# Attention, experts and feed-forward on one core: the two halves of a pair's weighted sum as one group, and the work before the first scores spread over other engines

## The chip, the core and the metric

The kernel runs on one core of a Trainium2 chip. A core has TensorE (PE, matmuls, and transposes as matmuls with the identity; its weight loads are shown as PEld), VectorE (DVE), ScalarE (ACT), GpSimd (POOL) and SyncE (SP, which here only issues DMAs). Each engine works through its own row of instructions in order and waits at semaphores for the others. Matmul results go to PSUM, eight banks of 2 KB in each of 128 partitions. The metric is the device time of one execution in microseconds, less is better. It is about 0.2% exact for this kernel.

## What is computed

Inputs are q, k, v of shape 4 x 8 x 576 x 64 (batch, heads, positions, head size) and s of 4 x 8 x 576, all float32. Cut to what matters:

```python
cum = np.cumsum(np.maximum(s, 0.0), axis=-1)
bias = np.minimum(-(cum[:, :, :, None] - cum[:, :, None, :]), 0.0)
scores = np.where(causal, -1e9, q @ k.transpose(0, 1, 3, 2) / 8 + bias)
attn = np.exp(scores - scores.max(-1, keepdims=True))
x = (attn / (attn.sum(-1, keepdims=True) + 1e-9)) @ v      # attention
x = x.transpose(0, 2, 1, 3).reshape(2304, 512)
e = argmax(x @ w_gate)             # one of 8 experts for each row of x
y = gate_w * sigmoid(x @ w_output_gate)[e] * (relu(x @ w1[e]) @ w2[e])
out = relu(y @ w_in)**2 @ w_out    # a third feed-forward layer
```

## The kernel before

Attention goes through 16 pairs of heads, four pairs to a batch. The 576 positions are four blocks of 128 rows and a tail of 64. A pair has seven units of work, which the list `order=[0, 1, 3, 11, 2, 10, 4]` puts into a row: units 0 and 1 are the first and the second row block of both heads, 2 and 3 the third and fourth block of the first head, 10 and 11 those of the second head, and 4 is the tail of both heads (the "tail scores", in a PSUM tile `s2` of two banks; all the others have tiles of one bank). Each unit goes through the same steps: scores on PE (`emit_s`, L635), bias, mask and the row maximum in one VectorE instruction (`emit_m`, L662), exp and row sum on ScalarE (`emit_e`, L679), transposes of the probabilities on PE (`emit_t`, L695, tile `t`), and a copy of them to SBUF on ScalarE or VectorE (`emit_v`, L714 and L716), into `pt0` for rows 0 to 255 and `pt1` for the rest.

Then comes the weighted sum with v, `emit_pv` (L732), which puts the two heads side by side (64 output partitions each, the form 128*64 in the profile). Half 0 sums the rows 0 to 255 over two blocks of keys: per head 256 and 128 columns. Half 1 sums the other 320 rows over five blocks: three times 320, then 192 and 64 columns. A float32 matmul shows as two instructions. Each half has a PSUM bank of its own from the ring of three banks that the transposes use too (tag `t`). ScalarE copies each half out (`emit_ov`, L743, into `oT`), VectorE makes the reciprocals of the row sums (`emit_rc`, L759 and L761), PE transposes the result back (`emit_xt`, L770), and VectorE scales it (`emit_xe`, L805) into a buffer that is stored to DRAM as x (`store_x`, L870 and L874).

Meanwhile the next pairs are prepared: q and k are loaded by six DMAs for each pair (L511, L514), transposed in three parts on PE (`qk_pe`, L548 and L550), converted to a high half on ScalarE (`qk_hi`, L575) and a low half on VectorE (`qk_lo`, L579), copied on GpSimd, and moved to the upper partitions by DMAs (L583). From the third pair on the bias comes in as extra rows of the scores' operands, read from the DRAM buffer `aug_d` (L538). The first two pairs add it by a fourth matmul with `cum_k` and `cum_q`, four slices that are made at the start from the cumulative sum (L1177 on ScalarE, L1179 on VectorE). Once a batch the gate's logits are made by `emit_lm` (L827), half by half, and the steps of the choice of the expert (L896 to L944) run between the attention steps of the following pairs.

The order of all this on each engine is written out by hand: `at(key, fn, ...)` puts a step into a list that is sorted by its key, in units of one seventh of a pair, and the table `K_` has the keys. `pv=[[3.74, 3.87], [8.47, ...]]` places half 0 in the middle of the next pair's units and half 1 near the end of them. The other keys that matter here are those of the copy after a half (`ov`), of its reciprocals (`rc`), of its transposes (`xt`), its scaling (`xe`), the store (`sx`) and the logits (`lt`).

Of the kernel before, what the change touches and what calls it, by code (L numbers as in the profile page):

```python
# [12 lines left out]
F32 = mybir.dt.float32  # L13
# [11 lines left out]
P = 128  # L25
# [17 lines left out]
    lt=[[-0.37, -0.33, 0.07, 0.12], [-0.22, 0.14, 0.64, 0.96]],  # L43
# [17 lines left out]
    pv=[[3.74, 3.87], [8.47, 8.49, 8.51, 8.53, 8.57]],  # L61
# [6 lines left out]
    sx=2.42,  # L68
# [22 lines left out]
def attention_moe_ffn_kernel(  # L91
# [359 lines left out]
    with tc.manual_schedule():  # L451
        with ExitStack() as actx:
# [34 lines left out]
            pt0 = [apool.tile([P, 2, 2, 256], F32, name=f"pt0{a}") for a in range(K_["ptb"])]  # L487
# [18 lines left out]
            def load_qk(pp):  # L506
                b, j = divmod(pp, HP)
                t = raw_q[pp] = qk_p.tile([P, 2 * QM + 2 * D], F32, tag="qk", name="qk")
                for i, src in enumerate((q, k)):
                    for hd in range(2):  # L510
                        nc.sync.dma_start(  # L511
                            out=t[:, i * QM:(i + 1) * QM].rearrange("p (r h d) -> p r h d", h=2, d=D)[:, :, hd],
                            in_=src[b, 2 * j + hd, 0:S - TAIL, :].rearrange("(r p) d -> p r d", p=P))
                    nc.sync.dma_start(  # L514
# [183 lines left out]
            def emit_v(pp, u, act):  # L698
                pb = pp % K_["ptb"]
                j0 = 0  # L700
                for i, (tp, n) in enumerate(t_t.pop((pp, u))):
                    if u < 2:
                        src = tp[:, 0:n * P].rearrange("p (h j i) -> p h j i", h=2, i=P)
                        dst = pt0[pb][:, :, 0:u + 1, u * P:(u + 1) * P]
# [15 lines left out]
            def emit_pv(pp, half, jbs):  # L720
                vt = raw_v[pp]
                if jbs[0] == 0:
                    o_t[pp, half] = ps_o.tile([P, 512], F32, tag=o_tag, name=o_tag)
                o = o_t[pp, half]
                last = 1 if half == 0 else NB - 1
                pt = (pt0 if half == 0 else pt1)[pp % K_["ptb"]]
                n = 256 if half == 0 else S - 256
                base = 0 if half == 0 else 2
                for jb in jbs:
                    c0 = max(jb - base, 0) * P  # L730
                    for hd in range(2):
# [3 lines left out]
                            rhs=pt[:, hd, jb, c0:n],  # L735
# [15 lines left out]
            def emit_rc(pp, half):  # L751
# [4 lines left out]
                b0, b1 = (0, 2) if half == 0 else (2, NB)  # L756
# [350 lines left out]
            with tc.tile_pool(name="prep", bufs=1) as prep:  # L1107
# [21 lines left out]
                nc.vector.tensor_copy(out=mask[:, 3 * P:4 * P], in_=mf)  # L1129
                for hd in range(2):  # L1130
                    r = slice(64 * hd, 64 * hd + 64)
                    nc.vector.tensor_copy(out=mask_t[r, S - TAIL:S], in_=mf[r, 64 * hd:64 * hd + 64])
# [8 lines left out]
                nc.scalar.copy(out=st_a[0][64:128, 0:3:2], in_=zf[64:128].unsqueeze(1).to_broadcast([64, 2, S]))  # L1141
                nc.vector.tensor_reduce(
# [34 lines left out]
                nc.scalar.activation(out=cum_q[:, 0], in_=cum_r.bitcast(F32), func=AF.Copy, scale=sel[:, 0:1])  # L1177
                for r in range(1, 2 * ND):
                    nc.vector.tensor_scalar(  # L1179
# [640 lines left out]
```

## Time and profile before

| | us |
|---|---|
| median of 3 runs | 862.26 (862.01 to 862.64) |
| the profiled execution | 862.62 |
| its span, first to last instruction | 860.9 |
| TensorE busy in it | 841.9 (98%) |
| VectorE busy | 523.8 (61%) |
| ScalarE busy | 450.7 (52%) |
| GpSimd busy | 260.0 (30%) |

The profile is of one execution. The span and the runs differ by the start and the end of the program around it. Busy shares are means over very different stages: attention in the first quarter, where all engines work, and the experts and the feed-forward layer behind it, which are mostly matmuls.

### The profile page before, as it was taken

What the parts mean: (1) busy time and instruction counts of PE and PEld (TensorE: products, weight loads), DVE (VectorE), ACT (ScalarE), POOL (GpSimd) and SP (SyncE); (2) the same over time, 40 slices, a digit from 0 to 9 for tenths busy, and PEclk for the clock granted to TensorE, in tenths of its full rate; (3) what the DMA queues carried; (4) which work ended last, traced back from release to release, by engine and by line L of the source; (5) the groups of instructions that cost most, each with busy time, mean ns of one, the idle gap of its engine ahead of it and who ended that gap; (6) DMA issues with size and microseconds to landing.
All of it is one profiled execution on the core that took longest, in us unless ns stands there. A gap on an engine that the chain in (4) does not pass through costs nothing.

```text
span 860.9 us, 15163 instructions
## 1 busy us (share of the span) xinstructions
PE 841.9 (98%) x5412; PEld 747.3 (87%) x5412; DVE 523.8 (61%) x1186; ACT 450.7 (52%) x1008; POOL 260.0 (30%) x302
## 2 busy tenths in 40 slices
PE   7999999999999999999999999999999999999996
PEld 5877777767799999999999999999999999999995
DVE  8667778877767686777976667664233343232221
ACT  6688888887555556565655546443233232232221
POOL 4312335534216555567422232331001011001001
PEclk9999999999999999999999999999999999999998
DMA  6667677753187978999983433321010121001001
GB/s 155 143 154 156 137 182 175 170 138 101 53 287 247 246 241 264 252 283 273 301 240 105 147 110 110 91 93 62 11 63 37 37 75 38 1 1 37 0 1 40
DMA packets 113028, 113.14 MB, mean 131 GB/s; under 512 B 66033, under 2 KB 83953, under 8 KB 112946
## 3 DMA queue, kind: packets, MB, share of 16 engines
q1 hardware_dynamic: 106162, 96.97, 41.6%
q0 software_dynamic: 3664, 9.62, 3.2%
q10 hardware_dynamic: 3120, 5.51, 1.9%
q8 instruction: 45, 0.74, 0.4%
q14 instruction: 37, 0.30, 0.1%
HBM read 80.50 MB, written 23.32 MB: 121 GB/s over the span
## 4 chain that ended last, share of the span: by engine, by line
PE 56%; issue 30%; ACT 5%; DVE 4%; POOL 2%; DMA 1%; POOLq 1%; SPq 1%; ACTq 0%; DVEq 0%
PE z L1427 19%; PE z L1469 11%; PE z L1478 7%; PE t L732 5%; PE s L635 5%; PE t L695 4%; ACT p L679 2%; POOL out_dram L1537 1%; ACT sta L575 1%; PE z L333 1%; PE t L548 1%; ACT pt L714 1%; PE s L770 1%; POOLq L1545 1%; PE t L827 1%
## 5 line engine op out<-in xcount | busy, mean ns | idle before, releaser
L1427 PE MATMUL z<-xt,w 128*128 128x384 f32 (+6 forms) x1920 | 329.6, 320 | 0.1
L1427 PEld LDWEIGHTS z<-xt,w 128*128 128x128 f32 x1920 | 308.1, 188 | 9.0 <-DVE h L1438 0.4
L1478 PE MATMUL z<-w,h 128*128 128x512 f32 x864 | 214.9, 393 | 0.0
L1478 PEld LDWEIGHTS z<-w,h 128*128 128x128 f32 x864 | 160.7, 188 | 29.3
L1447 DVE SCALAR_TENSOR_TENSOR r<-z,r 128x384 f32<-128x384 f32 x96 | 53.3, 555 | 127.4 <-ACT r L1446 127.4
L1446 ACT ACTIVATE r<-z 128x384 f32<-128x384 f32 x96 | 47.2, 492 | 150.8 <-PE z L1427 149.7
L1469 PE MATMUL z<-h,w 128*128 128x304 f32 (+5 forms) x768 | 111.0, 293 | 0.2 <-DVE h L1438 0.2
L1469 PEld LDWEIGHTS z<-h,w 128*128 128x128 f32 x768 | 104.0, 189 | 0.6 <-DVE h L1438 0.4
L1395 POOL TENSOR_TENSOR cvm<-cvm,cva 128x512 f32<-128x512 f32 x32 | 44.2, 1381 | 168.1 <-DVE cva L1391 128.3
L1454 DVE TENSOR_TENSOR h<-r,h 128x384 fp32r<-128x384 f32 x96 | 61.0, 635 | 50.4 <-ACT h L1453 50.4
L1537 POOL DMA_INDIRECT out_dram<-ysb,tok_m x18 | 17.4, 969 | 245.5 <-ACT ysb L1524 183.2
L679 ACT ACTIVATE p<-p,nm 128x128 f32<-128x128 f32 (+3 forms) x144 | 84.2, 590 | 4.8 <-DVE nm L662 4.7
L1453 ACT CAST h<-r 128x384 fp32r<-128x384 f32 x96 | 49.3, 514 | 63.7 <-DVE r L1447 63.3
L662 DVE CUSTOM_DVE_ANT_0 p<-s,mask 128x128 f32<-128x128 f32 (+3 forms) x128 | 59.6, 485 | 29.3 <-PE s L635 28.2
L250 DVE TENSOR_TENSOR w<-stg,w 128x1024 fp32r<-128x1024 f32 x49 | 73.6, 1502 | 5.4 <-ACT w L246 5.4
L695 PE MATMUL t<-ident,p 128*128 128x128 f32 x400 | 69.3, 283 | 2.6 <-DVE sta L579 1.1
L246 ACT CAST w<-stg 128x1024 fp32r<-128x1024 f32 x49 | 51.4, 1049 | 20.0 <-POOL cvm L1396 17.3
L695 PEld LDWEIGHTS t<-ident,p 128*128 128x128 f32 x400 | 44.5, 141 | 18.8 <-ACT p L679 6.8
L596 POOL CAST stb<-sta 64x1152 fp32r<-64x1152 f32 x28 | 31.4, 1150 | 78.1 <-PE s L635 47.9
L1396 POOL TENSOR_TENSOR cvm<-cvs,cvm 128x512 f32<-128x512 f32 x32 | 54.1, 1690 | 2.5
L635 PE MATMUL s<-sta 128*64 128x288 f32 (+4 forms) x204 | 50.1, 343 | 3.4 <-DMA sta<-aug_d 1.2
L714 ACT COPY pt<-t 128x512 f32<-128x512 f32 (+1 forms) x94 | 47.0, 515 | 7.3 <-PE t L732 4.1
(242 smaller groups left out, 1022.8 us busy)
## 6 DMA issues: line engine op xcount, KB each, us to landing
stg<-in_moe_w_dram SPq DMA_DIRECT2D x42, 512.0 KB
cv<-in_moe_w_out_dram SPq DMA_DIRECT2D x16, 512.0 KB
stx<-in_moe_w_dram SPq DMA_DIRECT2D x14, 512.0 KB
cv<-in_moe_w_in_dram SPq DMA_DIRECT2D x14, 512.0 KB
xr<-yT_d SPq DMA_DIRECT2D x8, 768.0 KB
qk<-in_q_dram SPq DMA_DIRECT2D x32, 128.0 KB
qk<-in_k_dram SPq DMA_DIRECT2D x32, 128.0 KB
v<-in_v_dram SPq DMA_DIRECT2D x32, 128.0 KB
```

The source lines that it names most:

```text
L250: nc.vector.tensor_tensor(out=lo, in0=raw.pop(job), in1=hi.bitcast(F32), op=ALU.subtract)
L635: nc.tensor.matmul(ps[0:mw, d0:d0 + nn], lhsT=ql[r, m0:m0 + mw], rhs=kl[r, c0:c0 + nn], start=(i == 0 and (tail or n == 0)), stop=(done an ...
L662: nc.vector.tensor_tensor_reduce(out=dst, in0=src, in1=msk, scale=-1.0, scalar=3.0e38, op0=ALU.add, op1=ALU.min, accum_out=nm[:, c:c + 1])
L679: nc.scalar.activation(out=pt[:, cs], in_=pt[:, cs], func=AF.Exp, scale=-1.0, bias=nm[:, c:c + 1], accum_out=rs[:, r:r + 1])
L695: nc.tensor.transpose(tp[:, i * P:(i + 1) * P], pt[:, j0:j0 + P], ident)
L714: nc.scalar.copy(out=dst, in_=src)
L1396: nc.gpsimd.tensor_tensor(out=m, in0=sq, in1=m, op=ALU.add)
L1427: nc.tensor.matmul(ps[:, 0:n], lhsT=wa[:, zw, kk, fl * P:(fl + 1) * P], rhs=xt[:, zx, kk, 0:n], start=(i == 0), stop=(i == 3 * KD - 1))
L1447: nc.vector.scalar_tensor_tensor(out=gg, in0=ps[:, 0:TT], scalar=0.0, in1=gg, op0=ALU.max, op1=ALU.mult)
L1454: nc.vector.tensor_tensor(out=ht[:, 1], in0=gg, in1=ht[:, 0].bitcast(F32), op=ALU.subtract)
L1469: nc.tensor.matmul(y_acc[g][d][:, 0:n], lhsT=wb[:, zw, fl, d * P:(d + 1) * P], rhs=ht[:, zh, 0:n], start=(f == 0 and i == 0), stop=(f == n ...
L1478: nc.tensor.matmul(acc, lhsT=ht[:, zh, c * P:(c + 1) * P], rhs=wb[:, zw, fl, :], start=(first and i == 0), stop=(last and i == 2))
```

## The change

Three things are changed.

First, the weighted sum. For all pairs but the last, half 0 is summed directly before half 1, and both halves go into one tile of two banks, from the pool in which the tail scores have their tile (tag `s2`). The copies of both halves then follow each other, and the reciprocals of a pair are made in one go for all five blocks. Since `pt0` is now read later, there are two of them, used in turn, and each is packed: the pieces of 256 and 128 columns stand behind one another. The transposes of half 0's result are moved to the next pair (`x0=10.87`), the store follows both halves (`sx=3.9`), and the logits of both halves stand side by side (`lt`).

Second, the front. The three loads of the first pair's k are issued by ScalarE, not by SyncE. The casts that make the masks go from VectorE to ScalarE; of the four slices of `cum_q` ScalarE makes two, not one, GpSimd the other two, and VectorE, which made three, none.

Third, the low halves of the first pair's last part are made before the `cum_q` slices.

```diff
-    lt=[[-0.37, -0.33, 0.07, 0.12], [-0.22, 0.14, 0.64, 0.96]],
+    lt=[[-0.37, -0.33, 0.07, 0.12], [-0.36, 0.14, 0.64, 0.96]],
...
-    pv=[[3.74, 3.87], [8.47, 8.49, 8.51, 8.53, 8.57]],
+    x0=10.87,
+    pv=[[8.45, 8.46], [8.47, 8.49, 8.51, 8.53, 8.57]],
...
-    sx=2.42,
+    sx=3.9,
...
-            pt0 = [apool.tile([P, 2, 2, 256], F32, name=f"pt0{a}") for a in range(K_["ptb"])]
+            pt0 = [apool.tile([P, 2, 3 * P], F32, name=f"pt0{a}") for a in range(2)]
...
+                    eng = nc.scalar if i == 1 and pp == 0 else nc.sync
                     for hd in range(2):
-                        nc.sync.dma_start(
+                        eng.dma_start(
...
-                        src = tp[:, 0:n * P].rearrange("p (h j i) -> p h j i", h=2, i=P)
-                        dst = pt0[pb][:, :, 0:u + 1, u * P:(u + 1) * P]
+                        src = tp[:, 0:n * P].rearrange("p (h c) -> p h c", h=2)
+                        dst = pt0[pp % 2][:, :, u * P:(2 * u + 1) * P]
...
-                    o_t[pp, half] = ps_o.tile([P, 512], F32, tag=o_tag, name=o_tag)
+                    if pp == NPAIR - 1:
+                        o_t[pp, half] = ps_o.tile([P, 512], F32, tag=o_tag, name=o_tag)
+                    else:
+                        if half == 0:
+                            o_t[pp] = ps_2.tile([P, 1024], F32, tag="s2", name="s2")
+                        o_t[pp, half] = o_t[pp][:, 512 * half:512 * half + 512]
...
-                b0, b1 = (0, 2) if half == 0 else (2, NB)
+                b0, b1 = (0, 2) if half == 0 else (2 if pp == NPAIR - 1 else 0, NB)
...
-                nc.vector.tensor_copy(out=mask[:, 3 * P:4 * P], in_=mf)
-                for hd in range(2):
-                    r = slice(64 * hd, 64 * hd + 64)
-                    nc.vector.tensor_copy(out=mask_t[r, S - TAIL:S], in_=mf[r, 64 * hd:64 * hd + 64])
...
+                nc.scalar.copy(out=mask[:, 3 * P:4 * P], in_=mf)
+                for hd in range(2):
+                    r = slice(64 * hd, 64 * hd + 64)
+                    nc.scalar.copy(out=mask_t[r, S - TAIL:S], in_=mf[r, 64 * hd:64 * hd + 64])
...
-                nc.scalar.activation(out=cum_q[:, 0], in_=cum_r.bitcast(F32), func=AF.Copy, scale=sel[:, 0:1])
-                for r in range(1, 2 * ND):
-                    nc.vector.tensor_scalar(
-                        out=cum_q[:, r], in0=cum_r.bitcast(F32), scalar1=sel[:, r:r + 1], scalar2=None, op0=ALU.mult)
-                    if r == 1:
-                        qk_lo(0, 2)
+                qk_lo(0, 2)
+                for r in range(2 * ND):
+                    if r < ND:
+                        nc.scalar.activation(
+                            out=cum_q[:, r], in_=cum_r.bitcast(F32), func=AF.Copy, scale=sel[:, r:r + 1])
+                    else:
+                        nc.gpsimd.tensor_scalar(
+                            out=cum_q[:, r], in0=cum_r.bitcast(F32), scalar1=sel[:, r:r + 1], scalar2=None,
+                            op0=ALU.mult)
...
-                    at(tv + K_["rc"], emit_rc, pp, half)
+                    if end or half == 1:
+                        at(tv + K_["rc"], emit_rc, pp, half)
+                    if not end and half == 0:
+                        tv = tv - K_["pv"][0][-1] + K_["x0"]
+                        tx = tv + K_["xe"]
```

What stands where on the engines shows it best. PE's row in the middle of the third pair, before the change; half 0 is the two rows of L732 behind the tail scores and the first transposes of the next q and k (`stb` and `sta` hold k and q, `pt_154` is `pt0`, `v_142` the pair's v):

```order
L635 MATMUL s_865<-stb_138 128x288 x4
L635 MATMUL s_865<-sta_137 64x288 x4
L548 MATMUL t<-ident,qk 128x128 x4
L732 MATMUL t<-pt_154,v_142 64x256 x2
L732 MATMUL t<-pt_154,v_142 64x128 x2
L695 MATMUL t<-ident,p 128x128 x3
L635 MATMUL s<-sta_135 128x192 x2
```

The same place on PE in the changed kernel (its lines have moved by 2 to 10):

```order
L637 MATMUL s_856<-stb_138 128x288 x4
L637 MATMUL s_856<-sta_137 64x288 x4
L550 MATMUL t<-ident,qk 128x128 x4
L697 MATMUL t<-ident,p 128x128 x3
L637 MATMUL s<-sta_135 128x192 x2
```

Half 0 is gone from there. It stands some fifteen rows later on PE in the changed kernel, at the end of the same pair (`pt_154` and `pt_156` are `pt0` and `pt1`, `s_981` is the tile of two banks):

```order
L697 MATMUL t<-ident,p 128x128 x4
L637 MATMUL s<-sta_135 128x384 x2
L742 MATMUL s_981<-pt_154,v_142 64x256 x2
L742 MATMUL s_981<-pt_154,v_142 64x128 x2
L742 MATMUL s_981<-pt_156,v_142 64x320 x6
L742 MATMUL s_981<-pt_156,v_142 64x192 x2
L742 MATMUL s_981<-pt_156,v_142 64x64 x2
L697 MATMUL t<-ident,p 128x128 x4
```

Before, the group there had only the three rows with 320, 192 and 64 columns. ScalarE's row around the copy of half 0, in the second pair before the change:

```order
L679 ACTIVATE p,rs_157<-p,nm 128x384
L743 COPY oT_309<-t 128x256
L679 ACTIVATE p,rs_157<-p,nm 128x576
L575 ACTIVATE sta_136<-t 128x512
L714 COPY pt_155<-t 128x3x128
L679 ACTIVATE p,rs_156<-p,nm 128x128 x2
```

And ScalarE's row there in the changed kernel:

```order
L681 ACTIVATE p,rs_158<-p,nm 128x384
L681 ACTIVATE p,rs_158<-p,nm 128x576
L577 ACTIVATE sta_136<-t 128x512
L716 COPY pt_156<-t 128x3x128
L681 ACTIVATE p,rs_157<-p,nm 128x128 x2
```

The copy of half 0 no longer stands between the exp of the last units and the tail's; it follows half 1's group, next to the copy of half 1. SyncE's row at the start of the changed kernel, in which two rows with the first pair's k are gone between the first q and the second:

```order
L1119 DMA sq<-in_s_dram 32x576
L513 DMA qk<-in_q_dram 128x4x64 x2
L516 DMA qk<-in_q_dram 64x2x64
L513 DMA qk<-in_q_dram 128x4x64 x2
L516 DMA qk<-in_q_dram 64x2x64
L513 DMA qk<-in_k_dram 128x4x64 x2
```

Those loads are now the first rows on ScalarE, ahead of the load of its function table.

## Rows read from the trace of the kernel before

**Rows 1.** The page's first part: busy time, share of the span, instructions.

```profile
PE 841.9 (98%) x5412; PEld 747.3 (87%) x5412; DVE 523.8 (61%) x1186; ACT 450.7 (52%) x1008; POOL 260.0 (30%) x302
```

**Rows 2.** Timeline of PE in one pair: start, duration, operation, idle time before with releaser.

```profile
90.37 0.60 PE L548 MATMUL t<-ident,qk 128*128 128x128 f32 x4
90.89 0.87 PE L732 MATMUL t<-pt,v 128*64 128x256 f32 x8
91.69 0.55 PE L695 MATMUL t<-ident,p 128*128 128x128 f32 x3
...
92.51 0.60 PE L548 MATMUL t<-ident,qk 128*128 128x128 f32 x4
92.95 0.38 PE L770 MATMUL s<-ident,oT 128*128 128x128 f32 x2
93.16 0.49 PE L695 MATMUL t<-ident,p 128*128 128x128 f32 x3
...
96.31 0.92 PE L695 MATMUL t<-ident,p 128*128 128x128 f32 x4
...
97.51 2.27 PE L732 MATMUL t<-pt,v 128*64 128x320 f32 x20
99.72 0.66 PE L695 MATMUL t<-ident,p 128*128 128x128 f32 x4
...
101.26 0.78 PE L635 MATMUL s<-stb 128*128 128x288 f32 x4
```

**Rows 3.** Timeline of ScalarE in the same pair.

```profile
91.00 0.60 ACT L575 ACTIVATE sta<-t 128x512 fp32r<-128x512 f32 x1 [0.31 <-PE t L548]
91.81 0.37 ACT L743 COPY oT<-t 128x256 f32<-128x256 f32 x1 [0.21 <-PE t L732]
...
93.19 0.60 ACT L575 ACTIVATE sta<-t 128x512 fp32r<-128x512 f32 x1 [0.24 <-POOL sta L597]
...
95.63 0.53 ACT L679 ACTIVATE p<-p,nm 128x256 f32<-128x256 f32 x1
...
96.13 0.52 ACT L679 ACTIVATE p<-p,nm 128x256 f32<-128x256 f32 x1
```

**Rows 4.** Timeline of VectorE in the same pair.

```profile
90.67 0.76 DVE L662 CUSTOM_DVE_ANT_0 p<-s,mask_t 128x576 f32<-128x576 f32 x1 [0.50 <-PE s L635]
...
94.63 0.18 DVE L910 TENSOR_REDUCE ix<-cand 128x5 f32<-128x40 f32 x1
94.73 0.41 DVE L662 CUSTOM_DVE_ANT_0 p<-s,mask 128x256 f32<-128x256 f32 x1
```

**Rows 5.** Timeline of SyncE's DMA issues.

```profile
3.07 1.14 SPq L511 DMA_DIRECT2D qk<-in_k_dram  x2
...
4.91 1.15 SPq L511 DMA_DIRECT2D qk<-in_q_dram  x2
...
37.19 0.49 SPq L538 DMA_DIRECT2D sta<-aug_d  x1
```

**Rows 6.** Timeline of PE before the third pair's first scores.

```profile
39.17 0.55 PE L695 MATMUL t<-ident,p 128*128 128x128 f32 x3
40.95 0.52 PE L635 MATMUL s<-sta 128*128 128x192 f32 x2 [1.23 <-DMA sta<-aug_d]
```

**Rows 7.** Windows: us, busy of each engine, granted PE clock, DMA share, GB/s.

```profile
10.00:11.00 1.00, 0.65 (x6) 0.65 (x6) 1.00 (x2) 0.79 (x4) 0.94 (x7) 1.00 0.94 215
12.00:13.00 1.00, 1.00 (x7) 1.00 (x7) 1.00 (x2) 0.00 (x0) 0.94 (x2) 0.50 0.91 286
41.00:42.00 1.00, 1.00 (x9) 0.99 (x10) 0.26 (x3) 0.00 (x0) 0.00 (x0) 1.00 0.71 196
```

**Rows 8.** Timeline of PE in a later pair.

```profile
156.73 0.66 PE L548 MATMUL t<-ident,qk 128*128 128x128 f32 x4 [0.49 <-DVE sta L579]
```

**Rows 9.** Timeline of PE between the logit matmuls of a batch's two halves.

```profile
75.07 0.55 PE L770 MATMUL s<-ident,oTx 128*128 128x128 f32 x3
75.55 0.46 PE L827 MATMUL t<-oT,wp 128*32 128x320 f32 x2
```

**Rows 10.** Timeline of VectorE before the first masks.

```profile
11.78 2.11 DVE L1179 TENSOR_SCALAR cum_q<-cum_r,sel 128x576 fp32r<-128x576 f32 x2
```

More of the change, by code (lines that the diff above doesn't have):

```diff
@@ L509, in load_qk @@
                 for i, src in enumerate((q, k)):
+                    eng = nc.scalar if i == 1 and pp == 0 else nc.sync
                     for hd in range(2):
-                        nc.sync.dma_start(
+                        eng.dma_start(
                             out=t[:, i * QM:(i + 1) * QM].rearrange("p (r h d) -> p r h d", h=2, d=D)[:, :, hd],
                             in_=src[b, 2 * j + hd, 0:S - TAIL, :].rearrange("(r p) d -> p r d", p=P))
-                    nc.sync.dma_start(
+                    eng.dma_start(
                         out=t[i * TAIL:(i + 1) * TAIL, 2 * QM:].rearrange("p (h d) -> p h d", h=2),
@@ L722, in emit_pv @@
                 if jbs[0] == 0:
-                    o_t[pp, half] = ps_o.tile([P, 512], F32, tag=o_tag, name=o_tag)
+                    if pp == NPAIR - 1:
[4 more added lines that the diff above has]
+                        o_t[pp, half] = o_t[pp][:, 512 * half:512 * half + 512]
                 o = o_t[pp, half]
                 last = 1 if half == 0 else NB - 1
-                pt = (pt0 if half == 0 else pt1)[pp % K_["ptb"]]
                 n = 256 if half == 0 else S - 256
@@ L730, in emit_pv @@
                     c0 = max(jb - base, 0) * P
+                    if half == 0:
+                        pt = pt0[pp % 2][:, :, 2 * c0:n + c0]
+                    else:
+                        pt = pt1[pp % K_["ptb"]][:, :, jb, c0:n]
                     for hd in range(2):
@@ L734, in emit_pv @@
                             lhsT=vt[:, jb, hd, :],
-                            rhs=pt[:, hd, jb, c0:n],
+                            rhs=pt[:, hd],
                             start=(jb == 0), stop=(jb == last))
@@ L1176, in attention_moe_ffn_kernel @@
                         qk_lo(0, part)
-                nc.scalar.activation(out=cum_q[:, 0], in_=cum_r.bitcast(F32), func=AF.Copy, scale=sel[:, 0:1])
-                for r in range(1, 2 * ND):
-                    nc.vector.tensor_scalar(
-                        out=cum_q[:, r], in0=cum_r.bitcast(F32), scalar1=sel[:, r:r + 1], scalar2=None, op0=ALU.mult)
-                    if r == 1:
-                        qk_lo(0, 2)
+                qk_lo(0, 2)
[3 more added lines that the diff above has]
+                            out=cum_q[:, r], in_=cum_r.bitcast(F32), func=AF.Copy, scale=sel[:, r:r + 1])
+                    else:
+                        nc.gpsimd.tensor_scalar(
+                            out=cum_q[:, r], in0=cum_r.bitcast(F32), scalar1=sel[:, r:r + 1], scalar2=None,
+                            op0=ALU.mult)
                 nc.scalar.copy(out=tri, in_=mt)
```

## The prediction, made before the result was known

> **What bounds the kernel now.** I read the engine totals first: TensorE (PE) has work for 98% of the span [rows 1], so what counts is what PE does and the few places where it stops. The mixture-of-experts layer and the feed-forward layer behind attention are one unbroken run of PE, which the change doesn't touch; whatever moves the end of attention should reach the end of the kernel one for one. Inside attention I then read the PE timeline of one pair of heads in the middle [rows 2], and ScalarE's and VectorE's beside it [rows 3, 4]: PE is nearly full, and the others run through most of a pair without a pause, so that two of PE's steps wait for them a little. Last I read the start: SyncE's queue [rows 5], PE's one long stop [rows 6], and the clock [rows 7].
>
> **One group instead of two.** Nothing is computed less: the 8 matmuls of the first half go from 90.89 to a place directly before the 20 of the second half at 97.51 [rows 2]. What can go is the cost of starting and ending a group. The first group lasts 91.69 − 90.89 = 0.80 us, the second 99.72 − 97.51 = 2.21. By the shapes in the code these are 384 and 1216 columns per head, so a straight line through both gives 0.0017 us for a column and 0.15 us for a group by itself. One group of all 1600 columns then takes about 2.86 us, 0.15 less than both. Ahead of the first group there is more: the transposes of L548 take 0.52 us until the next instruction (90.37 to 90.89) where it is a group of the 64-column form, and 0.44 (92.51 to 92.95) where it isn't [rows 2]: 0.08. So 0.23 us of PE work go per pair, for certain.
>
> Whether the end gets them is another matter, because 0.80 us leave the middle of the pair and 2.86 − 2.21 = 0.65 us come to its end. The stretch between is not PE's alone. The transposes at 96.31 take 0.92 us where the same four take 0.66 at 99.72: they wait for an exp on ScalarE that ends at 96.65 [rows 2, 3]. I followed ScalarE back from there. Its copies and exps, some fifteen rows of which five stand here, are one chain from 91.00 on; the first item is set by the transposes of the next q and k at 90.37, which nothing in the change moves relative to the tail scores before them. In this chain stands the copy of the first half's result at 91.81 (0.37 us), which waits for the moved group (0.21 us idle before it), and the second conversion at 93.19 waits 0.24 us for transposes that stand behind the moved group too [rows 3]. With both gone I put that exp at about 0.7 us earlier (0.21 + 0.24 of waits and about 0.3 of the copy). The joined group then starts 0.7 us earlier and lasts 0.65 longer. **A pair whose limit is ScalarE gets about 0.07 us shorter**, not 0.23 and not 0.8.
>
> VectorE is the other half of that. In pairs that carry steps of the expert gate, four small operations stand in its row between the low halves and the second unit's masks (the last is at 94.63; the mask behind it starts 0.10 later, so they take some 0.4 us), and that mask ends at 95.14 [rows 4]. Its exp starts at 95.63 [rows 3] and, with the readout of the mask's minimum between them, could start at 95.3 at the earliest. ScalarE's gain there is cut from 0.7 to about 0.3, while the group still gets 0.65 longer: **such a pair gets about 0.33 us longer**. Of the pairs 2 to 14 (counted from 0, the last is 15) I count four in which VectorE is full in that way. In one more pair the conversion waits much longer behind the moved group (PE stops 0.49 us at 156.73, since ScalarE and VectorE come late from a weight cast and the copy) [rows 8]; there I take a gain of 0.3. The bounds for any one pair are a gain of 0.23 (PE alone decides) and a loss of 0.65 (exp and masks don't move at all).
>
> Sum over pairs 2 to 14: 8 × −0.07 = −0.56; 4 × +0.33 = +1.32; −0.3; together +0.46.
>
> **New waits.** The sums now stand in the two banks in which the next pair's tail scores are written, so those wait for both copies. The second copy is one row of 0.4 us directly behind the group; the tail scores come 1.5 us after it (99.72 against 101.26 in the pair shown) [rows 2]. The masks that read these banks end at 91.43 [rows 4], six us before the next group begins. I cost both at nothing; what hides them is the transposes and scores of the last units. If that cover went, ScalarE would have to be more than 1 us late at the end of a pair.
>
> **Side effects.** The reciprocals of a pair are made once instead of twice: two VectorE instructions fewer, off the path. The transposes of the first half's result stand at the same place one pair later, at the same cost. Its DRAM store follows later on SyncE's queue; nobody reads it before the experts. The copies into the packed buffer have the same size. For each of the four batches the gate's logit matmuls of both halves now stand side by side. That saves a change of form and back: three transposes of L770 last 0.48 us before the logits (75.07 to 75.55) [rows 9], against 0.21 us for two (92.95 to 93.16) [rows 2], so about 0.16 for the entry alone; I take 0.2 with the exit: 4 × −0.2 = −0.8.
>
> **The front.** The three loads of the first k leave SyncE's queue, two cum_q sums (2.11 us) [rows 10] and the mask casts leave VectorE, and the first scores should be 2 to 3 us earlier. That this counts I doubt. PE's longest stop in attention comes later: pair 2's first scores start at 40.95 after 1.23 us of waiting for the DMA of `aug_d` [rows 6], issued at 37.19 [rows 5], and SyncE issues almost without a pause from the start until then. What PE gains before is waited away here; what the wait gives back is what SyncE gains: the first k's three issues take 4.91 − 3.07 = 1.84 us of it [rows 5]. The bounds are 0 (the same bytes go through the same DMA engines, and loads on both queues may land no earlier) and −1.84; I take **−1.6**, near the upper end, because the row of issues behind is so dense. The Trainium skill says the same in "Trainium Kernel Development and Optimization", section Key Constraints: queues of several engines share the 16 DMA engines, and issuing from several saves only the sequencer's issue time. The 1.84 us are such issue time; no run here shows more yet. Pair 1's first half (0.80 us) stood just before that wait; behind it the joined group is 0.65 longer, with nothing given back: **+0.65**.
>
> **The sum**, against the profiled execution's 862.62 us: −1.6 + 0.65 + 0.46 − 0.8 = −1.29, so 861.33. The median of the runs is 0.36 below the profiled one, so I forecast **861.0 us**.
>
> **Rivals.** (B) PE alone decides: the waits at 96.31 and for the low halves are small, and ScalarE and VectorE have gained work room. Then every pair from 2 to 14 gives 0.23: −1.6 + 0.65 − 13 × 0.23 − 0.8 = −4.74, so 857.5. For it: PE's 98%. Against: the 0.92 us at 96.31 [rows 2], which show that ScalarE is on the path just before the second group. The Trainium skill's "TensorEngine Tiling (Array Packing)", section Key Properties, says that switching the tiling mode drains TensorE; by that rule one switch in and one out go per pair, which is this rival's result. The trace agrees that the edges cost something (0.15 and 0.08), not that they are all that counts.
>
> (C) Slower: exp and masks hold their times. If lo(q,k), the masks and the second unit's exp are set by VectorE's row in most pairs, PE idles in the hole that the first group leaves, and each of the 13 pairs gets longer by 0.65 less what ScalarE still gains, about 0.25: +0.4. −1.6 + 0.65 + 13 × 0.4 − 0.8 = +3.45, so 865.7. It decides once ScalarE's gain at that exp is under 0.42 us on the mean (0.65 − 0.23). For it: VectorE is without a pause from the low halves on in most pairs. Against: even in the pair shown, which has gate steps, the mask ends 0.49 us before its exp starts (95.14 to 95.63) [rows 3, 4], and without them it would be some 0.4 more.
>
> (D) The clock. From 10 to 11 us PE was busy for 0.65 of the time, and from 12 to 13 the granted clock was 0.50, the lower of its levels, 1.2 GHz [rows 7]. If PE reaches pair 2's scores earlier by the front's 2 to 3 us and the DMA by only 1.6, its stop there grows from 1.23 to some 2.5 us, and the clock could fall behind it. A microsecond or two at half clock costs about 1.2: 862.2. Against: from 41 to 42, right behind the stop of 1.23 us, it was 1.00 [rows 7]. The Trainium skill's "TensorE: Matmul & The Clock Gate" has idleness as the cause of the lower clock; the rows agree only for the front.
>
> **How the numbers follow.** My forecast 0.42, B 0.24, C 0.22, D 0.12. A measurement of this kernel can tell about 0.2% (1.72 us) from no change, so faster is below 860.54 and slower above 863.98. The forecast's own spread (SyncE 0 to −1.84, four gated pairs or two or six) splits it into 0.16 faster, 0.24 same, 0.02 slower; B is faster; C is 0.20 slower and 0.02 same; D is 0.10 same and 0.02 slower. Faster 0.40, same 0.36, slower 0.24. For 8 in 10 the range goes from 857.0 (just below B, which could bring more where gate-free waits vanish too) to 865.3 (into C).
>
> **What would show it.** In the changed profile: a joined group of 2.8 to 2.9 us per pair; its start about 9.1 us after the pair's transposes of 87.69 instead of 9.8 where no gate step runs, 9.5 with them; the copies of both halves back to back; pair 2's first scores at 39.1 to 40 after a stop of over 2 us; tail scores that wait for nothing. Wrong would be: groups with no wait before them and pairs of 11.8 (B), a new stop of PE before the second unit's transposes (C), granted clock under 1 after pair 2's stop (D), or pair 2's scores where they were (SyncE gains nothing).

## The result, and the profile after

The changed kernel takes 868.16 us (median of 4 runs, 867.71 to 869.6), the kernel before 862.41 beside it: a ratio of 1.0063, 95% interval 1.0049 to 1.0076. It is slower by 5.75 us, where 861.0 was forecast with a range up to 865.3.

The first part of the page of the changed kernel (busy time, share of the span and instructions of each engine) differs little from [rows 1]; PE has 2 us less work in a span of 865.9 us, 5.0 more than before:

```profile
PE 839.7 (97%) x5412; PEld 747.0 (86%) x5412; DVE 512.5 (59%) x1150; ACT 450.1 (52%) x1012; POOL 263.2 (30%) x304
```

So PE waits longer. What it waits for between 45 and 225 us, the attention from the third pair on, is the view of waits (waited for, us in total, times, longest). After, and then before:

```profile
PE t L697 <- DVE sta L581: 7.1, 15, 1.2
```

```profile
PE t L695 <- DVE sta L579: 1.1, 2, 0.7
```

L697 and L695 are the same line, the transposes of the probabilities; L581 and L579 are VectorE's low halves of the next q and k. This wait grew by 6.0 us; all waits of PE that this view lists for the stretch grew from 3.4 to 7.5. The waiting transposes need a PSUM bank: in the ring of three, they come by the code to the bank in which a part of q and k stands, and that bank is free only when its low half has been made. No run gives the ring a fourth bank.

To see where the 5.0 us of the span come from, I measured from the end of one pair's second-half group to the next in the timeline. In parts: up to the third pair's first scores −1.96; from there to the end of the second pair's group +0.56; pairs 2 to 14 +3.99; the last pair up to the first expert's first matmuls (they are for the 128 of its tokens that are gathered early) −0.20; from there to its matmuls for the other tokens +1.90; the rest +0.71.

The front did what it was to do at the queue, and little more. SyncE's issue, PE's stop, and the windows (us, busy of PE, PEld, DVE, ACT, POOL, granted clock, DMA share, GB/s) in the changed kernel:

```profile
35.27 0.49 SPq L540 DMA_DIRECT2D sta<-aug_d  x1
```

```profile
38.99 0.44 PE L637 MATMUL s<-sta 128*128 128x192 f32 x2 [1.32 <-POOL sta L599]
```

```profile
12.00:13.00 1.00, 1.00 (x5) 0.90 (x5) 1.00 (x4) 0.39 (x3) 0.90 (x2) 0.50 0.80 185
...
38.00:40.00 2.00, 1.01 (x9) 1.04 (x10) 0.92 (x6) 0.87 (x2) 1.69 (x4) 1.00 0.51 114
```

The issue of `aug_d` is 1.92 us earlier than in [rows 5], the scores 1.96 earlier than in [rows 6]. By the profile the stop now ends with GpSimd's memset (L599) and no longer with the DMA, so it is in part chance that the two numbers lie so close. The clock falls to its lower level at the start as it did in [rows 7], and stays at full behind the stop.

### The profile page after: what moved, and what is told of

Same layout as the page of the kernel before. It is cut to its first block, busy times and chain, and to the rows that moved or that the text cites. A ratio compares the mean times of both kernels' runs of the same rounds, so it can differ in the third digit from the quotient of the medians.

```text
span 865.9 us, 15121 instructions
## 1 busy us (share of the span) xinstructions
PE 839.7 (97%) x5412; PEld 747.0 (86%) x5412; DVE 512.5 (59%) x1150; ACT 450.1 (52%) x1012; POOL 263.2 (30%) x304
## 4 chain that ended last, share of the span: by engine, by line
PE 56%; issue 29%; ACT 5%; DVE 4%; POOL 2%; DMA 1%; POOLq 1%; SPq 0%; ACTq 0%; DVEq 0%
PE z L1444 19%; PE z L1486 11%; PE z L1495 7%; PE s L742 5%; PE s L637 5%; PE t L697 4%; ACT p L681 2%; POOL out_dram L1554 1%; DVE sta L581 1%; PE z L334 1%; PE t L550 1%; ACT pt L716 1%; PE s L780 1%; ACT sta L577 1%; POOLq L1562 1%
## 5 line engine op out<-in xcount | busy, mean ns | idle before, releaser
L697 PE MATMUL t<-ident,p 128*128 128x128 f32 x400 | 69.4, 283 | 8.6 <-DVE sta L581 7.1
L697 PEld LDWEIGHTS t<-ident,p 128*128 128x128 f32 x400 | 44.6, 141 | 23.7 <-DVE sta L581 12.8
```

What stands on the lines that cost most here:

```text
L697: nc.tensor.transpose(tp[:, i * P:(i + 1) * P], pt[:, j0:j0 + P], ident)
```

## The chain in one pair, before and after

The view of the chain (start, us, what the end of the stretch hung on) shows what took the gain. In the pair whose gate step makes the one-hot rows (`r`), in the changed kernel, from the transposes of the next q and k to the joined group:

```profile
102.18 0.45 PE t L550 x4
...
102.65 0.44 ACT sta L577
103.09 1.13 DVE r L954
104.22 0.60 DVE sta L581
104.82 0.47 DVE pt L718
...
105.93 0.33 DVE xs L815
106.27 0.61 DVE sta L581
...
106.92 0.44 PE t L697 x2
...
109.74 2.86 PE s L742 x28
```

And in the kernel before, the same pair:

```profile
102.57 0.44 PE t L548 x4
103.00 0.80 PE t L732 x8
103.80 0.48 PE t L695 x3
104.28 0.43 PE s L635 x4
104.71 0.45 PE t L548 x4
...
105.16 0.54 DVE pt L716
...
106.69 0.61 DVE sta L579
107.34 0.44 PE t L695 x2
...
110.16 2.21 PE t L732 x20
```

Before, half 0 (0.80) is itself a link of the chain, and while PE works on it and on the transposes and scores behind it, ScalarE makes the high half and VectorE the gate step and the first low half, unseen. From L548 to the group are 7.59 us. After, the 0.80 are gone, and what lay under them is the chain: the high half, the gate step, the first low half, everything on VectorE up to the second low half, and only then the tail's last two transposes. From L550 to the group are 7.56 us. Nothing is gained, and the group is 2.86 instead of 2.21: the pair takes 13.26 us instead of 12.57.

The gate step in this chain is not long by itself. The same instruction takes 0.31 us elsewhere in this pair (at 105.62); here it takes 1.22, and it ends 0.1 us after two copies on GpSimd have ended:

```profile
101.87 2.23 POOL L598 CAST stb<-sta 64x1152 fp32r<-64x1152 f32 x2 [6.08 <-ACT pt L716]
```

```profile
103.00 1.22 DVE L954 TENSOR_SCALAR r<-iota_r,rk_all 128x384 bf16<-128x384 f16 x1
```

So part of what half 0 covered is a wait of VectorE for GpSimd. The last section shows that it is not the only one.

A pair without gate steps in that stretch, changed kernel:

```profile
63.13 0.45 PE t L550 x4
...
64.29 0.70 DVE sta L581
...
65.04 0.56 PE t L697 x3
...
67.60 1.10 ACT p L681 x4
...
69.54 2.86 PE s L742 x28
```

Here the chain leaves VectorE after the first low half, for unit 10's transposes and ScalarE. From L550 to the group are 6.41 us; before they were 7.05 in the same pair (64.37 to 71.42), so 0.64 are gained, 0.65 are lost in the group, and the pair takes 12.11 instead of 12.03. The rest, some 0.07, is a small new wait: the transposes of half 1's result now stand behind two copies instead of one. ScalarE's two copies in one row and the transposes L780, which take 0.39 us until the next instruction where before they took 0.32:

```profile
99.38 0.70 ACT L753 COPY oT<-s 128x256 f32<-128x256 f32 x2 [1.85 <-PE s L742]
```

## The experiments

Times scatter more in these series than in the first, mostly by the wait for `aug_d` and by PE's stops at the start of the experts. (In the profiled executions that have the front of before, the third pair's first scores start at 40.03, 40.95 and 41.85 us.) So beside the ratio I give what can be compared to about 0.05 us: the time from group end to group end in the profiled execution, for a pair without gate steps, the first pair with logits, the first pair that chooses experts, the first with one-hot rows, a later one that chooses, and the sum of all 13 (pairs 2 to 14).

| kernel | ratio to before (95%) | none | logits | choice | one-hot | later choice | sum of 13 |
|---|---|---|---|---|---|---|---|
| before | | 12.03 | 14.13 | 12.03 | 12.57 | 12.66 | 162.93 |
| changed | 1.0063 (1.0049 to 1.0076) | 12.11 | 14.50 | 12.43 | 13.26 | 13.37 | 166.92 |
| e1_front | 0.9981 (0.9970 to 0.9993) | 12.04 | 14.14 | 12.03 | 12.57 | 12.65 | 162.89 |
| e2_group | 1.0086 (1.0066 to 1.0106) | 12.11 | 14.50 | 12.43 | 13.25 | 13.38 | 166.87 |
| e3_mem | 1.0039 (1.0025 to 1.0053) | 12.12 | 14.50 | 12.43 | 13.27 | 13.37 | 166.85 |
| e4_pad | 1.0015 (1.0005 to 1.0026) | 12.03 | 14.13 | 12.04 | 12.55 | 12.66 | 162.91 |
| e5_lo_after_mask | 1.0068 (1.0048 to 1.0088) | 12.12 | 15.13 | 12.44 | 12.69 | 13.38 | 168.17 |
| e6_lo_before_mask | 1.0153 (1.0140 to 1.0167) | 13.46 | 15.83 | 13.46 | 13.45 | 13.46 | 177.23 |
| e7_front_lo | 1.0011 (1.0001 to 1.0022) | 12.04 | 14.80 | 12.03 | 12.61 | 12.65 | 165.29 |
| e8_front_logits | 0.9995 (0.9986 to 1.0003) | 12.02 | 14.56 | 12.03 | 12.57 | 12.66 | 164.21 |
| e9_logits_back | 1.0062 (1.0044 to 1.0081) | 12.10 | 14.79 | 12.43 | 13.26 | 13.38 | 167.75 |
| e11_scale_later | 1.0058 (1.0038 to 1.0079) | 12.09 | 14.76 | 12.25 | 12.95 | 13.65 | 167.22 |
| e12_copy_scalar | 1.0031 (1.0019 to 1.0044) | 12.18 | 14.32 | 12.18 | 12.80 | 12.93 | 165.78 |
| e10_front_scale | 0.9969 (0.9958 to 0.9980) | 12.03 | 14.12 | 12.04 | 12.30 | 12.94 | 162.63 |

**The front and the groups apart.** First the front alone; the edits of the diff from `load_qk` and the masks on, and nothing of `emit_pv`:

```diff
+                    eng = nc.scalar if i == 1 and pp == 0 else nc.sync
...
+                nc.scalar.copy(out=mask[:, 3 * P:4 * P], in_=mf)
...
+                    if r < ND:
+                        nc.scalar.activation(
```

> The kernel before with only the front of the change (first k on ScalarE's queue, mask casts and two cum_q slices on ScalarE, the other two on GpSimd); the weighted sums stay in two groups. Theory (the front gives SyncE's queue 1.6 us and nothing else): about 860.8 us, 1.3 to 2.0 less than before, third pair's first scores at 39.0 to 39.6 instead of 40.95 after a stop of more than 2 us. Rival (the front is worth nothing, since loads on two queues land no earlier): 862.4. Rival (the front itself costs, by a lower clock behind the longer stop): 863 or more.

861.27 us beside 863.22: 1.95 less, as the theory had it. The third pair's first scores start at 38.75, in this run without a stop, since PE was later there than I had thought: the granted clock was 0.50, its lower level, from 11 to 14 us here too. Then the other half, the changed kernel with those edits undone:

> The changed kernel without its front: joined groups only. Theory (the whole loss comes from the joined groups and what goes with them, the front gains): 869.5 to 870.2 us, that is 7 to 8 above before. Rival (part of the loss is the front's): 867 or less, and the kernel with the front alone is then slower than before.

870.67 us, 7.45 more than before. The two parts add up to the whole change (7.45 − 1.95 = 5.5, measured 5.75): the front gains, the joined groups and what came with them lose. That the sum fits so well is in part chance, for the six runs of this kernel lie between 868.73 and 873.69. The profiled one is the slowest, and it shows something that the other profiles don't: behind a stop of 3.48 us the granted clock fell to 0.50 and was back at 1.00 from 46 us on.

```profile
41.85 0.44 PE L636 MATMUL s<-sta 128*128 128x192 f32 x2 [3.48 <-DMA sta<-aug_d]
```

```profile
43.00:44.00 1.00, 1.00 (x7) 1.00 (x6) 0.28 (x3) 0.58 (x1) 0.00 (x0) 0.50 0.88 182
```

**The place of a buffer.** The changed kernel's stop of PE at the first expert, and ScalarE's conversion of the tokens (`xt`) that it waits for:

```profile
243.42 1.60 PE L1444 MATMUL z<-xt,w 128*128 128x224 f32 x12 [1.18 <-ACT xt L1354]
```

```profile
242.40 0.97 ACT L1354 CAST xt<-z 128x512 fp32r<-128x512 f32 x2 [5.83 <-PE z L1108]
```

The transposes of these tokens were done at 237.3, and ScalarE was idle; it waited 5.83 us for matmuls that don't make or use them: L1108 is the first expert's work on its 128 early tokens. The two packed buffers take 6 KB per partition where one of 4 KB stood. That makes attention's pool 2 KB longer, and the tokens, which are laid into freed memory, now overlap its end by 1256 bytes. ScalarE's first write there waits until the pool is free, and the matmuls on the early tokens still read operands that stand in it (`sta`). Two kernels test it. The changed kernel with the second buffer elsewhere:

```diff
-            pt0 = [apool.tile([P, 2, 3 * P], F32, name=f"pt0{a}") for a in range(2)]
+            pt0 = [apool.tile([P, 2, 3 * P], F32, name="pt00")]
...
+            pt0.append(l_p.tile([P, 2, 3 * P], F32, name="pt01"))
```

> The changed kernel with the second packed buffer put into another SBUF pool, so that the first expert's transposed tokens lie where they lay before. Theory (the 2 KB more in attention's pool make these tokens overlap it, and their conversion on ScalarE then waits until the last matmuls that read attention's pool are done, which PE pays with its stop of 1.18 us and a little behind it): 866.3 to 867.0 us, and the conversion starts right after the transposes of the tokens. Rival (the stop at the experts' begin comes from the later stores of x and so the later gather): 868.2, the stop stays.

And the kernel before with 2 KB more that nobody uses:

```diff
+            pt0 = [apool.tile([P, 1536], F32, name="pt00")[:, 0:1024].rearrange("p (h j i) -> p h j i", h=2, j=2)]
```

> The kernel before with 2 KB per partition added to the first half's buffer and never used; nothing else differs. Theory (it is the place in SBUF alone): the first expert's conversion waits for the last matmuls on attention's pool, PE stops 1.1 to 1.3 us there, 863.6 us, 1.0 to 1.5 above before. Rival (the overlap costs only together with the later end of attention): 862.4, no stop.

ScalarE's conversion in the changed kernel with the buffer elsewhere, and then in the kernel before with the dead 2 KB:

```profile
237.58 0.58 ACT L1355 CAST xt<-z 128x512 fp32r<-128x512 f32 x1 [1.14 <-PE z L334]
```

```profile
238.31 0.97 ACT L1337 CAST xt<-z 128x512 fp32r<-128x512 f32 x2 [5.13 <-PE z L1098]
```

The wait goes with the first edit and comes with the second, with the same stop of 1.18 us on PE. The ratios agree: 0.24% less (2.1 us) for the one, 0.15% more (1.45 us between the medians) for the other. So this part is shown: dead memory alone makes the kernel slower. The stop for the gathered tokens before it stayed (0.99 us with the buffer elsewhere, 0.74 in the changed kernel, 0.15 before). The gather starts 4.33 us after the last store of x was issued in the changed kernel, and 3.70 before; in the profiles of the kernels with joined groups it is 4.1 to 4.7, in those without 3.1 to 3.9. Why was not tried and stays open.

**First theory: the first low half.** PE waits for L581, so let it come sooner. From here on all kernels with joined groups have the buffer elsewhere.

```diff
+                        soon = pp >= 5 and part == 0
-                        at(tq + K_["qkh"], qk_hi, pp, part)
-                        at(tq + K_["qkl"], qk_lo, pp, part)
+                        at(tq + (0.265 if soon else K_["qkh"]), qk_hi, pp, part)
+                        at(tq + (0.27 if soon else K_["qkl"]), qk_lo, pp, part)
```

> The changed kernel with the second packed buffer in the other pool, and from the sixth pair on with the low half of a pair's first q and k part directly behind the tail's mask in VectorE's row. In five pairs (three with logits, two with the gate's one-hot rows) this takes a gate step of 0.5 to 0.8 us from ahead of it; nothing else is moved there, but for two weight casts on ScalarE. Theory (in the joined kernel unit 10's transposes wait for a PSUM bank until that low half is made, so a gate step ahead of it costs PE time one for one): the wait of the transposes for the low halves falls from 7.1 us to 4 or less, and the time by 1.5 to 2.5 us against the same kernel without the move (866.4 on the chip where before took 863.2). Rival (ScalarE's chain sets these pairs as my forecast had it, and VectorE's masks behind are then late by the same gate steps): under 0.5 us of difference.

The wait of the transposes for low halves fell from 7.1 to 3.9 us, as expected, and the time did not follow. The first pair with one-hot rows went from 13.27 to 12.69, but the pairs with logits went from 14.50 to 15.13, and the second pair with one-hot rows stayed. The gain in the one-hot pair is the collision with GpSimd: behind the low half its gate step takes 0.23 us, where it took 1.13.

```profile
103.31 0.69 DVE sta L581
104.00 0.23 DVE r L954
```

In the pairs with logits the wait had moved on: where the logits' reduction (0.80 us) no longer stands ahead of the first low half, it stands ahead of the second. The theory falls in this form. With 0.25 and 0.255 in the place of 0.265 and 0.27:

> As the run with the low half behind the tail's mask, but ahead of this mask, in eleven pairs. Theory (the transposes of unit 10 wait for the low half): their wait falls to 2 us or less of 7.1; the tail's mask comes 0.6 to 0.7 us later and takes some of it back through its exp; 1.5 to 4 us less than without the move, and less than the run with the low half behind the mask. Rival (ScalarE's chain sets the pairs): the exp of the tail and all behind it come 0.6 us later, and the kernel is 1 to 5 us slower than without the move.

1.5% slower, against the theory, and by far more than the rival had; all pairs without logits take 13.4 to 13.5. ScalarE's and VectorE's rows in a pair without gate steps:

```profile
65.19 0.60 ACT L577 ACTIVATE sta<-t 128x512 fp32r<-128x512 f32 x1 [0.30 <-PE t L550]
```

```profile
65.88 0.69 DVE L581 SCALAR_TENSOR_TENSOR sta<-t,sta 128x512 fp32r<-128x512 f32 x1 [1.89 <-POOL stb L598]
66.49 0.75 DVE L664 CUSTOM_DVE_ANT_0 p<-s,mask_t 128x576 f32<-128x576 f32 x1
```

The view names GpSimd's copy as what the low half waited for, but the first of the two copies had ended at 65.41 and the second ends at 66.50, while ScalarE's high half ended at 65.79, right before the low half. By the code, too, the copy is of another pair's operands. So the low half can't come earlier than its high half, and with the tail's mask behind it VectorE is idle for 1.89 us and the mask comes late too. This says nothing for or against the chain on VectorE; it tells why the low half stands where it stands. The control, the first of these two moves in the kernel with the front alone:

> The kernel with the front alone, and with the same move of the low half behind the tail's mask as a control: here half 0 still stands between the q and k transposes and unit 10's. Theory (half 0's 0.8 us cover VectorE's low half, so nothing waits for it): 861.3 on the chip where before took 863.2, the same as without the move within 0.7 us. Rival (the gate steps ahead of the low half cost in both kernels): 1.5 us less or more.

863.79 us beside 863.11, slower than the front alone, against the theory; by pairs only those with logits (14.80 instead of 14.14) and one more changed. In the others half 0 does cover the low half, as the theory had it.

**The logits.** In the front kernel, `lt` of the change:

```diff
-    lt=[[-0.37, -0.33, 0.07, 0.12], [-0.22, 0.14, 0.64, 0.96]],
+    lt=[[-0.37, -0.33, 0.07, 0.12], [-0.36, 0.14, 0.64, 0.96]],
```

> The kernel with the front alone, and with the logits of both halves side by side as in the change. Forecast's term (0.2 us for each of four batches): 0.8 us less than the front alone, 860.5 where before took 863.2. Rival (the logits' side-by-side place makes a later step of VectorE stand ahead of the low half, and gives nothing): 861.3 or more.

The three pairs with logits take 0.42, 0.36 and 0.48 us longer: transposes wait for VectorE to read the logits out of their PSUM banks (2.2 us in four waits). The saving of the forecast is not there. I concluded that this edit costs in the changed kernel too, and undid it there:

> The changed kernel with the second packed buffer in the other pool, and the logits of a batch's second half back at their place of before (behind the transposes of that half). Theory (putting the logits side by side costs, as in the kernel with the front alone, where the three pairs with logits went from 14.14, 14.27, 14.14 to 14.56, 14.63, 14.62 us from group end to group end): the three pairs with logits take 14.1 to 14.2 us instead of 14.50, all others as without the edit; 865.2 where before took 863.1. Rival (the joined group makes them longer, the place of the logits doesn't matter): they stay at 14.5, 866.4.

That fell as well. The pairs with logits went up, from 14.50 to 14.79. With joined groups the side-by-side logits help by 0.29; without them they hurt by 0.42. A joined group by itself costs the first and the third of these pairs 14.79 − 14.14 = 0.65, the whole length that it grew by, and the second 0.53.

**Second theory: VectorE's whole row.** Not one operation but the sum of VectorE's work between the first high half and the second low half sets the pairs with gate steps. (Not those with logits: in the changed kernel their chain leaves VectorE behind the first low half and goes on over ScalarE, as in a pair without gate steps.) Then taking any 0.3 to 0.5 us from that stretch must shorten them, and only them. First the scaling of half 0's transposed result, moved behind the masks:

```diff
-                        tx = tv + K_["xe"]
+                        tx = tv + K_["xe"] + 0.65
...
-    sx=3.9,
+    sx=4.35,
```

> As the run with the logits back, and VectorE's scaling of the first half's transposed result (0.34 us) moved from ahead of the low half of the second q and k part to behind the masks that follow it. Theory (in pairs with gate steps VectorE's row from the first to the second low half sets the time, one for one): pairs of 12.43, 13.26, 13.37, 13.47 and 12.28 us get 0.3 to 0.35 shorter, those of 12.11 and 12.05 don't change by more than 0.1; 863.6 to 864 where before took 863.1. Rival (ScalarE's chain sets them): no pair gets shorter. Rival (the score banks that the transposed result keeps longer are missing): pairs get longer by 0.2 or more.

Three of the five got shorter, by 0.18, 0.31 and 0.28; two got longer (13.38 to 13.65, 12.28 to 12.43); pairs without gate steps stayed. Mixed: the work is only moved to where the next masks need VectorE. Then the copy of unit 2's probabilities, given to ScalarE:

```diff
-    vact=[[0], [1], [1], [1], [0], [1], [1, 1]],
+    vact=[[0], [1], [1], [1], [1], [1], [1, 1]],
```

> As the run with the logits back, and the copy of unit 2's transposed probabilities (0.47 us) on ScalarE instead of VectorE. Theory (gated pairs hang on VectorE's row, the others on the low half and then on ScalarE): the pairs of 12.43, 13.26, 13.37 and 13.47 us get 0.3 to 0.47 shorter, the pairs of 12.11 and 12.05 0.2 to 0.5 longer, since their chain runs through ScalarE behind the low half; in all 864.5 to 866.5. Rival (ScalarE sets all pairs): every pair 0.3 to 0.5 longer, 870 or more.

The pairs of 13.26 and 13.38 got 0.46 and 0.45 shorter, that of 12.43 got 0.25 shorter, those with logits 0.47, 0.09 and 0.46; those of 12.10 and 12.06 got 0.08 and 0.12 longer. The fourth of the expected ones (13.44) did not move. Its trace shows why: the copy's 0.46 us are gone there too, but a gate step behind them now stands where GpSimd makes a weight's low half (156.83 to 158.11), and what took 0.60 us without the edit takes 1.06 with it:

```profile
159.02 0.60 DVE L954 TENSOR_SCALAR r<-iota_r,rk_all 128x384 bf16<-128x384 f16 x1
```

```profile
157.16 1.06 DVE L954 TENSOR_SCALAR r<-iota_r,rk_all 128x384 bf16<-128x384 f16 x1
```

Over the 13 pairs it is 1.97 us less. The chain in the pair with one-hot rows shows the 0.47 gone from its place and nothing put there:

```profile
102.57 1.14 DVE r L954
103.71 0.59 DVE sta L581
104.30 0.20 DVE p L664
...
105.28 0.61 DVE sta L581
```

So ScalarE is not what holds these pairs; more work on it makes them shorter. The rival that ScalarE sets all pairs is out. The edit has its price: PE's wait for low halves is 2.6 us now, but it waits 2.7 us for ScalarE's copies, and the first pair that chooses experts has its chain on ScalarE.

**A version that beats both.** The front alone, and the later scaling:

> The kernel with the front alone, and the same later scaling of the first half's result. Theory (also with half 0 in its old place three pairs with gate steps, 12.57, 12.65 and 12.75 us, hang on VectorE's row before the second low half): these three get 0.3 shorter, the rest stay; 860.4 where before took 863.1, against 861.3 for the front alone. Rival (there the row has slack or the banks are missing): 861.3 or more.

862.16 us beside 864.28, a ratio of 0.9969 (0.9958 to 0.9980), against 0.9981 for the front alone. Of the three pairs that the theory named the first, with one-hot rows, gains 0.27, the second loses 0.29 and the third stays; a late pair gains 0.43, so by pairs the scaling is worth only 0.26 us in all; that it is better than the front alone is within the intervals. Both beat the kernel before.

## Why the prediction was wrong

It named the place and took the wrong engine's row. By its own steps:

- **The group.** 2.86 us were forecast for the joined group and 0.65 more than half 1 alone; the chain shows 2.86 and 0.65. Right.
- **Pairs without gate steps.** Forecast −0.07, measured +0.08. The exp chain came 0.64 earlier instead of 0.7, and the copies of both halves, which were cost at nothing, hold the next transposes by 0.07. A size, not a mechanism. In two later pairs (+0.26 and +0.33) these copies, put at nothing, are the first link of the chain; one pair near the end, with no new q and k to prepare, got 0.29 shorter.

```profile
203.97 0.70 ACT oTx L753 x2
```

- **Pairs with gate steps.** This step failed. It let the exp behind the masks come 0.3 us earlier, by [rows 3, 4], and so put a pair at +0.33 and counted four of them. It never followed the second low half to the tail's last transposes: in the one-hot pair the chain ran over it already before. That stretch did not get shorter (7.59 and 7.56 us), so the pair pays the group's 0.65 and a little more. Three pairs pay 0.69 to 0.72 (the two with one-hot rows and a later one that chooses experts), the first that chooses pays 0.40, and the three with logits, which the count left out, 0.37, 0.22 and 0.37. The pair of [rows 2] to [rows 4] is the one with 0.40; +0.33 was forecast for it, and that this is near is luck, for its chain runs over VectorE's row up to the second low half and not over the mask and its exp. The one pair for which [rows 8] promised a gain of 0.3 lost 0.72. Forecast for pairs 2 to 14: +0.46 without the logits, −0.14 with the three batches whose logits fall into them; measured +3.99. Rival C had the price nearly right (0.4 a pair) with the right reason, VectorE's row, and the stop of PE ahead of transposes that was named as its sign came (7.1 us in all); what I held against it was the slack of one mask before its exp, which is not the slack of the chain.
- **The logits.** Forecast −0.8 from [rows 9]. On PE alone the edit does save: 1.59 us for both halves and the transposes between them, against 1.73 before. But PE is not alone there. The edit is worth −0.29 in the first pair with logits beside joined groups and +0.42 without them.
- **The front.** Forecast −1.6 up to the third pair's scores and +0.65 for the second pair; measured −1.96 and +0.56. Right in size, and right that the first scores don't count: they came some 0.9 us earlier (the transposes behind them at 14.03 instead of 14.90), not 2 to 3. In the execution of e3_mem, where the granted clock was 1.00 from 8 to 17 us, these transposes start at 13.25, and the third pair's scores still at 38.93. That SyncE's 1.84 us alone are the reason is not shown: its issue did come 1.92 earlier, but the stop then ended with GpSimd, and in e1_front there was none.
- **Rival D.** It did not come in the changed kernel: the stop was 1.32 us, not the 2.5 that was forecast for it, and the granted clock behind it was 1.00. As a mechanism it is not out: in e2_group the stop was 3.48 us, and the clock behind it fell to 0.50.
- **Rival B.** One group instead of two saves 0.15 us of PE, and that is not the bound. For such an edge the Trainium skill has a reason in "TensorEngine Tiling (Array Packing)", section Key Properties: changing the tiling mode drains TensorE. The 0.15 us agree with it, but no run here shows that they are a drain.
- **Not thought of.** The prediction let the end of attention reach the end of the kernel one for one, and so put the experts' start at nothing; that step failed too. It is 1.90 us longer: the second buffer's 2 KB, which cost a stop of 1.18 us and by the runs 1.5 to 2 us, and the later gather (0.6). The buffers stood in the diff; I asked what they hold and not what will lie on them afterwards.

From the forecast's −1.29 us to the 5.0 by which the span grew are 6.3: 3.5 in pairs 2 to 14, 0.8 that the logits were to save, 1.9 at the first expert, and terms that nearly cancel.

## What to carry to other kernels

Work that stands in the middle of an engine's row may be the cover for a chain on two other engines; before it is moved, follow that chain from where it starts to where it comes back (here q and k, high half, low half, transposes), because its length is what is left when the cover is gone. Slack at one wait is not the slack of the row: when a low half came sooner, the next one was late. A link of the chain that is longer than the same instruction elsewhere is worth a look at what the other engines do just then. And a buffer that grows in one stage can shift what later stages lie on; a dead 2 KB showed it.

## What was not expected of the hardware

The same small VectorE comparison, 128 x 40, takes 0.20 us in one pair and 1.15 in another, in the kernel before as in the changed one (1.13 there), and in the second pair it stands in the chain:

```profile
93.28 0.20 DVE L901 TENSOR_TENSOR eq<-lg,mx 128x40 f32<-128x40 f32 x1
```

```profile
144.19 1.15 DVE L901 TENSOR_TENSOR eq<-lg,mx 128x40 f32<-128x40 f32 x1
```

The trace shows what it meets: GpSimd makes a weight's low half just then, and the comparison ends 0.05 us after that.

```profile
144.00 1.29 POOL L273 TENSOR_TENSOR w<-stg,w 128x512 fp32r<-128x512 f32 x1
```

It is not this one alone. From 40 to 225 us, 16 VectorE instructions of the kernel before take over 0.15 us longer than the fastest of the same line and shape, 11 in the changed kernel and 8 to 19 in the others. Every one starts while a GpSimd instruction runs and ends 0.02 to 0.12 us after it. All of them read SBUF only; none of the masks, copies and low halves, which read PSUM, is among them. No run moves GpSimd's work, so this rests on the traces, and on the two edits above that moved a VectorE step out of such a place and into one.

From the end of the last pair's group to the end of the last matmul, where all these kernels run the same code, the profiled executions took from 629.5 to 635.2 us; PE's stops there, for h and for the gathered tokens, came and went with edits that lie hundreds of microseconds ahead. Why is open.
